# Second-layer weights combined on chip, one block product spread over the pairs, and pairs in another order

## The chip, the cores and the metric

The kernel runs on one core of a Trainium2 chip. The metric is the device time of one execution in microseconds (us); the time before is the median of three runs.

## What is computed

The reference chains three blocks on inputs of 4 batches with 576 positions each. Only the last one is touched by the change.

```python
def _moe2_ref(x, g_ln, w_ch1, w_ch2):          # x: (4, 576, 512)
    mu = np.mean(x, axis=-1, keepdims=True)
    var = np.mean((x - mu) ** 2, axis=-1, keepdims=True)
    xn = (x - mu) / np.sqrt(var + 1e-06) * g_ln
    ch = np.maximum(xn @ w_ch1, 0.0) @ w_ch2   # (512, 2048) and (2048, 512)
    return (x + ch).astype(np.float32)
```

Ahead of it come attention (8 heads, four of them with a local mask of 32 positions, four with a strided one) and a gated block with its own two products, `_attn_ref` and `_moe_ref`.

## The kernel before

**Stages.** The first 302 us are attention and the gated block, batch by batch. In the last batch, the hooks `PREP_AT` and `NORM0_AT` already prepare weights and normalise the first columns of the channel block. Then `last_stage` does the channel block in three thirds of 768 columns (`sc` = 0, 1, 2), each cut into two halves of 384 columns (`TH`).

**Precision.** Every f32 operand of a matmul is split in two parts, high and low (`split`: ScalarE writes the high part, VectorE the rest), and each product takes three matmuls, low by high, high by low, high by high.

**The first layer** is not done as eight block products of 2 by 2 blocks but as seven, on sums and differences of blocks (`expand` makes those of x, `combine` those of the weights). One pass is a *pair* i = 0 to 7: seven products of 6 matmuls each. In the first two thirds, `pair` does them in the order 1, 7, 6, 2, 5, 3, 4. Products 1, 6, 5 and 3 add up in one PSUM bank `a`, and ScalarE copies that bank out in between (`s1` after 1, `u2` after 6, `u4` after 5, `late(f1)` after 3): so product 6 waits for the copy `s1`, 5 for `u2`, 3 for `u4`. Bank `b` takes 7 and then 4, which waits for VectorE to have read 7 (`late(f2)`, L899); bank `c` takes 2. Three banks of a ring of four serve a pair.

**The second layer** of the first two thirds is `ch2`: 4 blocks of 3 matmuls, 12 for each f = 0 to 15. The first half's `ch2` are mixed into the pairs, the second half's follow as a loop of 16 on what `late` keeps. In the last third, `last_pair` only makes the sums (`hb`), and `last_chunk` does the second layer as seven block products too, of 48 matmuls each, in the order `ORDER2`; `grain` splits the inputs of a product, `fetch2` loads its two weight slices of 1024 KB, `out2` takes its results out.

**Weights.** `prepare(n)` runs the next n units of a list: `piece` loads and converts a quarter of the weights of one i (`from_f64`, in the staging tile `stg`), `combine` makes the seven sums of the first layer's weights and splits them into the tile `w1`, `second` splits the second layer's into `w2`, and `store2` writes the f32 copy of the latter to DRAM (`w2f_scratch`). `keep` writes `w1` to DRAM for the other two thirds, `fetch` reads it back into one of two tiles, used in turn. During the second third `combine2(i)` reads the f32 copy back into `stg`, makes the sums (L681 to L684), splits them and writes both parts to DRAM (L688) for `fetch2`.

**Order.** All loads and stores go through SyncE's one queue. The framework plans each engine's order when the kernel is built, from an estimate of costs and from who waits for whom, so an engine's order in the trace is near that of the source but not the same: what is ready may be drawn forward. On the chip each queue is then in that order.

Of the kernel before, what the change touches and what calls it, by code (L numbers as in the profile page):

```python
# [24 lines left out]
P = 128  # L25
# [19 lines left out]
WX2 = {1: (0, 2, 0), 2: (4, 2, 2), 7: (1, 2, 1), 4: (5, 2, 2), 5: (8, 1, 0), 6: (10, 1, 1), 3: (12, 1, 3)}  # L45
ORDER2 = (1, 2, 7, 6, 5, 4, 3)
XTAGS = (0, 4, 1, 5, 2, 3, 6)
# [104 lines left out]
def mixer_kernel(ctx: ExitStack, tc: tile.TileContext, io, out):  # L152
    nc = tc.nc
    y_d = nc.dram_tensor("y_scratch", (KD, P, NT), F32, kind="Internal").ap()
    w_d = nc.dram_tensor("w_scratch", (len(PRE), P, WP), F32, kind="Internal").ap()
    w2f_d = nc.dram_tensor("w2f_scratch", (NW, P, 2 * DM), F32, kind="Internal").ap()
    w2_d = nc.dram_tensor("w2_scratch", (14, P, NW, 2, P), F32, kind="Internal").ap()
# [511 lines left out]

    def store2(i):  # L670
        nc.sync.dma_start(out=w2f_d[i], in_=big["stg"][:, 2048:3072].bitcast(F32))

    def combine2(i):
        stg = big["stg"]
        c = stg[:, 0:1792].bitcast(F32)
        wf = c[:, 0:1024].rearrange("p (k e r f) -> p k e r f", k=2, e=2, r=2)
        nc.sync.dma_start(out=c[:, 0:1024], in_=w2f_d[i])
        s = c[:, 1024:1792].rearrange("p (s e f) -> p s e f", s=3, e=2)
        a11, a21, a12, a22 = wf[:, 0, :, 0], wf[:, 0, :, 1], wf[:, 1, :, 0], wf[:, 1, :, 1]
        tt = nc.vector.tensor_tensor  # L680
# [24 lines left out]
    for i in range(NW):  # L705
# [5 lines left out]
        if i + 1 < NW:  # L711
            units += [(combine, (i + 1,))]
        units += [(store2, (i,))]
    done = [0]
# [49 lines left out]
    def norm(sc, step, role):  # L764
# [21 lines left out]
        if step < 5:  # L786
            srs[sc] = col_sum(sc, (step - 1) % 2, step > 2)
        else:
            for k in range(KD):
                nc.scalar.activation(yc[:, k, :], yc[:, k, :], AF.Copy, scale=g_2[:, k:k + 1])  # L790

# [87 lines left out]
    def pair(sc, i, role, mid):  # L879
# [7 lines left out]
        product(sc, i, b, 7, True)  # L887
        product(sc, i, a, 6, False)
        u2 = tmp("u2")
        nc.scalar.activation(u2, a, AF.Copy)  # L890
        c = bank(role, "ps_p2")[:, :TH]
        product(sc, i, c, 2, True)
        c11 = tmp("c11")
        tt(out=c11, in0=c, in1=s1, op=ALU.add)
        h1 = to_h(c11)
        product(sc, i, a, 5, False)
        u4 = tmp("u4")
        nc.scalar.activation(u4, a, AF.Copy)
        tt(out=late(f2), in0=b, in1=u4, op=ALU.add)  # L899
        if i:  # L900
            ch2(sc, 0, f1 - 2, 1 - role)
        mid()
        product(sc, i, a, 3, False)
        nc.scalar.activation(late(f1), a, AF.Relu)
# [3 lines left out]
        h2 = to_h(c21)  # L908
        if i:
            ch2(sc, 0, f2 - 2, 1 - role)  # L910
# [7 lines left out]
    def last_stage():  # L918
        for sc in range(NSC - 1):
            role = sc % 2  # L920
            for i in range(NW):
                pair(sc, i, role, lambda: steps_at(sc, i - 0.5, role))
                if sc == 0:
                    if i + 2 < NW:
                        prepare(len(units[done[0]:]) if i + 3 == NW else 7)
                        if i < NW - 2:
                            keep(i + 2)
                else:
                    if i + 2 < NW:
                        fetch(i + 2)  # L930
                    combine2(i)
                steps_at(sc, i, role)
# [10 lines left out]
            for f in range(NF):  # L943
# [3 lines left out]
                if f == 4:  # L947
                    residual(sc, 1)
                ch2(sc, 1, f, role)
            for d in range(KD):  # L950
# [8 lines left out]

    def last_pair(sc, i, b):  # L960
        tt = nc.vector.tensor_tensor
        relu = lambda dst, src: nc.scalar.activation(dst, src, AF.Relu)
        a = bank8("ps_p1")[:, :TH]
        product(sc, i, a, 1, True)
        s1 = tmp("s1")
        nc.scalar.activation(s1, a, AF.Copy)
        o = bank8("ps_p6")[:, :TH]
        product(sc, i, o, 6, True)
        u2 = tmp("u2")
        tt(out=u2, in0=o, in1=s1, op=ALU.add)  # L970
        product(sc, i, a, 2, False)
        relu(b[:, 0], a)
        d = bank8("ps_p7")[:, :TH]
        product(sc, i, d, 7, True)
        u3 = tmp("u4")
        tt(out=u3, in0=d, in1=u2, op=ALU.add)
        c = bank8("ps_p5")[:, :TH]
        product(sc, i, c, 5, True)
        tt(out=b[:, 3], in0=c, in1=u3, op=ALU.add)
        relu(b[:, 3], b[:, 3])  # L980
        e = bank8("ps_p4")[:, :TH]
        product(sc, i, e, 4, True)
        tt(out=b[:, 2], in0=u3, in1=e, op=ALU.add)
        relu(b[:, 2], b[:, 2])
        product(sc, i, c, 3, False)
        tt(out=b[:, 1], in0=c, in1=u2, op=ALU.add)
        relu(b[:, 1], b[:, 1])

# [16 lines left out]
    def last_chunk(sc):  # L1005
# [3 lines left out]
        for i in range(NW):  # L1009
# [8 lines left out]
            b = hb[g][:, i % 2]  # L1018
            last_pair(sc, i, b)
            x = first_a[:, 2 * i:2 * i + 2] if 2 * i < NLATE else first_b[:, 2 * i - NLATE:2 * i - NLATE + 2]  # L1020
# [6 lines left out]
            if i + 2 < NW:  # L1027
                fetch(i + 2)
            if i in (1, 3):
                fetch2(i // 2)  # L1030
            if i == NW - 3:
                residual(sc, 0)
            if i >= NW - 2:
                rsqrt(sc, i + 2 - NW)
        pair_tile = lambda: big["h"].tile([P, 2, TH], F32R, tag="h", name="pt").bitcast(F32)
        ps, s1, u2, u3 = {}, pair_tile(), pair_tile(), pair_tile()
        for n, m in enumerate(ORDER2):
            if n + 1 < len(ORDER2):
                for e in range(2):
                    fetch2(2 * n + 2 + e)  # L1040
                for g in range(NW // 2):
                    grain(ORDER2[n + 1], g)
            onto = {2: 1, 3: 5}.get(m)
            for e in range(2):
                ps[m, e] = ps[onto, e] if onto else bank8("ps_c")[:, :TH]
            order = [(i, e) for i in range(NW) for e in range(2)]
            if n + 1 == len(ORDER2):
                order.sort(key=lambda ie: ie[1])
            for i, e in order:
                w, x = slices[m, e], grans[m, i]  # L1050
                for k, (a, c) in enumerate(((1, 0), (0, 1), (0, 0))):
                    nc.tensor.matmul(ps[m, e], lhsT=w[:, i, a, :], rhs=x[:, c, :], start=not onto and i == 0 and k == 0,  # L1052
                                     stop=i == NW - 1 and k == 2, skip_group_check=True)
                if i == NW - 1:
                    out2(sc, m, e, ps[m, e], s1[:, e], u2[:, e], u3[:, e])

    p7 = {}

    def out2(sc, m, e, o, s1, u2, u3):
        tt = nc.vector.tensor_tensor  # L1060

        def finish(half, r, src):
# [126 lines left out]
    open_d()  # L1189
    prepare(max(0, 14 - done[0]))  # L1190
    keep(1)
# [18 lines left out]
```

## Time and profile before

| | us |
|---|---|
| median of 3 runs (lowest, highest) | 695.57 (693.05, 697.37) |
| the profiled execution: its time, its span | 693.15, 691.0 |
| PE busy, PEld busy | 660.8, 626.8 |
| DVE busy, ACT busy | 507.7, 376.1 |
| mean share of the DMA queue in its 16 engines | 63.3% |

PE is TensorE's matmuls, PEld its weight loads, DVE VectorE, ACT ScalarE, SP SyncE with the DMA queue. The span is the time from the first to the last instruction; some 2 us of the execution's time lie around it. A matmul's row shows its whole way through the array, so that PE counts as busy also where one matmul starts later than it could; the spacing of starts tells more.

### The profile page before, as it was taken

Reading aid. Unit: us, or ns where it says so; the run is one execution under the profiler, and the core shown is the slowest. Engines: PE = TensorE matmul, PEld = TensorE weight load, DVE = VectorE, ACT = ScalarE, POOL = GpSimd, SP = SyncE. Lnnn points to the kernel's source line nnn. Section 1 sums busy time; section 2 is a strip of 40 time slices with the busy share of each in tenths; the row PEclk is TensorE's granted clock in tenths of the full one; section 3 lists DMA queues with packets and bytes.
Section 4 is the critical chain, followed back from the end, with each engine's and each line's share of the span. In section 5 each row is a group of like instructions: output and inputs, shape, how many; then the busy total and the mean of one; then the engine's idle time right before and its main releaser. Section 6 shows DMA issues by size and latency. Waiting matters only on the chain.

```text
span 691.0 us, 12856 instructions
## 1 busy us (share of the span) xinstructions
PE 660.8 (96%) x5002; PEld 626.8 (91%) x5002; DVE 507.7 (73%) x1026; ACT 376.1 (54%) x884; POOL 19.8 (3%) x24
## 2 busy tenths in 40 slices
PE   5899999999999998999999799989999999999997
PEld 4689989989888988999999699989999999999997
DVE  4889786586758686997798994564669757659683
ACT  3988967283568347646567743333476325445340
POOL 0011020000200020000000000000000000000000
PEclk9999999999999999999999999999999999999999
DMA  8863233557451650458978957799768869564753
GB/s 266 290 195 114 83 99 112 158 157 223 149 157 47 204 171 1 168 206 318 376 285 319 345 203 231 229 328 314 244 225 291 267 211 349 215 229 176 269 223 138
DMA packets 68235, 148.33 MB, mean 215 GB/s; under 512 B 4496, under 2 KB 43664, under 8 KB 63312
## 3 DMA queue, kind: packets, MB, share of 16 engines
q1 hardware_dynamic: 68176, 147.53, 63.3%
q8 instruction: 39, 0.64, 0.4%
q14 instruction: 20, 0.16, 0.1%
HBM read 101.90 MB, written 45.61 MB: 213 GB/s over the span
## 4 chain that ended last, share of the span: by engine, by line
PE 55%; DVE 15%; DMA 13%; ACT 11%; issue 3%; POOL 1%; SPq 1%; DVEq 0%; ACTq 0%; POOLq 0%
PE ps_p L833 19%; PE ps_c L1052 7%; PE ps_o L208 4%; PE ps_o L209 4%; PE ps_o L210 4%; DMA w<-w_scratch 2%; DMA w_scratch<-w_p 2%; ACT pt L405 2%; DMA qk<-in_qk_l 2%; DMA w_scratch<-stg 2%; DMA stg<-in_w_ch 2%; PE ps_y L208 2%; PE ps_y L210 1%; PE ps_y L209 1%; PE ps_t L444 1%
## 5 line engine op out<-in xcount | busy, mean ns | idle before, releaser
L833 PE MATMUL ps_p<-x,w 128*128 128x384 f32 x1008 | 187.8, 339 | 8.3 <-DVE w L185 3.6
L833 PEld LDWEIGHTS ps_p<-x,w 128*128 128x128 f32 x1008 | 175.1, 189 | 14.8 <-DVE w L185 3.9
L209 PE MATMUL ps_o<-h,w2p 128*128 128x384 f32 x192 | 64.3, 335 | 0.0
L210 PE MATMUL ps_o<-h,w2p 128*128 128x384 f32 x192 | 64.2, 334 | 0.0
L208 PE MATMUL ps_o<-h,w2p 128*128 128x384 f32 x192 | 62.3, 335 | 0.4 <-ACT h L838 0.4
L1052 PE MATMUL ps_c<-t,w2c 128*128 128x384 f32 x288 | 50.5, 335 | 1.1 <-DMA w2c<-w_scratch 1.0
L1052 PEld LDWEIGHTS ps_c<-t,w2c 128*128 128x128 f32 x288 | 49.9, 188 | 1.7 <-DMA w2c<-w_scratch 1.3
L208 PE MATMUL ps_g<-wsg,vn 128*128 128x288 f32 x128 | 39.0, 305 | 0.0
L210 PE MATMUL ps_g<-wsg,vn 128*128 128x288 f32 x128 | 38.2, 299 | 0.0
L208 PE MATMUL ps_u<-xhl,winl 128*128 128x288 f32 x128 | 38.1, 297 | 0.0
L208 PE MATMUL ps_y<-gt,wout 128*128 128x288 f32 x128 | 37.9, 298 | 0.1
L209 PE MATMUL ps_g<-wsg,vn 128*128 128x288 f32 x128 | 37.9, 296 | 0.0
L209 PE MATMUL ps_u<-xhl,winh 128*128 128x288 f32 x128 | 37.8, 295 | 0.0
L210 PE MATMUL ps_u<-xhl,winh 128*128 128x288 f32 x128 | 37.7, 295 | 0.0
L210 PE MATMUL ps_y<-gt,wout 128*128 128x288 f32 x128 | 37.5, 295 | 0.0
L209 PE MATMUL ps_y<-gt,wout 128*128 128x288 f32 x128 | 37.5, 294 | 0.0
L208 PEld LDWEIGHTS ps_o<-h,w2p 128*128 128x128 f32 x192 | 35.8, 188 | 0.7 <-ACT h L838 0.7
L209 PEld LDWEIGHTS ps_o<-h,w2p 128*128 128x128 f32 x192 | 36.0, 188 | 0.4 <-DVE h L839 0.2
L210 PEld LDWEIGHTS ps_o<-h,w2p 128*128 128x128 f32 x192 | 36.1, 188 | 0.0
L838 ACT ACTIVATE h<-late 128x384 fp32r<-128x384 f32 x32 | 16.7, 524 | 35.1 <-PE ps_o L210 30.5
L184 ACT ACTIVATE t<-hb 128x768 fp32r<-128x768 f32 x24 | 20.2, 846 | 23.5 <-PE ps_c L1052 23.0
L208 PE MATMUL ps_v<-winh,xhl 128*128 128x512 f32 x80 | 31.9, 399 | 0.3 <-DVE xhl L500 0.2
(225 smaller groups left out, 1574.4 us busy)
## 6 DMA issues: line engine op xcount, KB each, us to landing
w<-w_scratch SPq DMA_DIRECT2D x16, 1792.0 KB, 7.7
w_scratch<-w SPq DMA_DIRECT2D x8, 1792.0 KB, 7.6
w_scratch<-stg SPq DMA_DIRECT2D x16, 896.0 KB, 6.3
w2c<-w_scratch SPq DMA_DIRECT2D x14, 1024.0 KB, 6.2
stg<-in_w_ch SPq DMA_DIRECT2D x22, 512.0 KB, 6.0
raw_p<-in_w_ch SPq DMA_DIRECT2D x20, 256.0 KB, 3.1
qk<-in_qk_s SPq DMA_DIRECT2D x8, 601.0 KB, 4.5
y_scratch<-y SPq DMA_DIRECT2D x16, 288.0 KB, 3.1
```

The lines of the kernel that those rows point to most:

```text
L184: nc.scalar.activation(dst_h, src, AF.Copy)
L208: nc.tensor.matmul(ps, lhsT=ll, rhs=rh, start=first, stop=False)
L209: nc.tensor.matmul(ps, lhsT=lh, rhs=rl, start=False, stop=False)
L210: last_mm[0] = nc.tensor.matmul(ps, lhsT=lh, rhs=rh, start=False, stop=last)
L405: exps.append(nc.scalar.activation(p3[:, i, :], src, AF.Exp, scale=SCALE, bias=mx[:, i:i + 1], accum_out=sm[:, i:i + 1]))
L444: nc.tensor.transpose(ps[:rows, (t - t0) * c:(t - t0 + 1) * c], src, ident)
L833: nc.tensor.matmul(o, lhsT=w[:, a, n0 + nk * k, :], rhs=x[:, c, k, :], start=first and k == 0 and n == 0, stop=k == 1 and n == 2, skip_gro ...
L838: nc.scalar.activation(h[:, 0, :], src, AF.Relu)
L1052: nc.tensor.matmul(ps[m, e], lhsT=w[:, i, a, :], rhs=x[:, c, :], start=not onto and i == 0 and k == 0, stop=i == NW - 1 and k == 2, skip_g ...
```

## The change

It has five parts. (1) `w2f_scratch` and `store2` are gone; `combine2` adds the high and the low part of `w2[i]` on VectorE instead of loading the sum; as `store2` was one unit of seven in each step, `prepare` counts 6 and 13. `combine2(7)` moves from pair 7 of the second third into the loop of its second half, at f = 12 (`COMBINE_F`). (2) `pair` takes the products in the order 1, 7, 2, 6, 5, 3, 4 and puts one `ch2` before 5 and the other before 3, in place of one before 3 and one after 4; in pair 7 the second stays at the end. (3) `last_pair` takes the scheme of `pair`, with one bank for four products. (4) In the last third, block product 1 of the second layer is no longer a stage of 48 matmuls but goes in 6 at a time, inside the next pair (`mid`, between 5 and 3); the stage after it is product 7, whose slices come one after the other, then 2. Banks come from `bank6`, and `fetch2(0)` and `fetch2(1)` stand after pair 0. (5) The scaling by `g_2` in the first third's normalisation goes from ScalarE to VectorE.

```diff
-ORDER2 = (1, 2, 7, 6, 5, 4, 3)
+COMBINE_F = {12: 7}
+ORDER2 = (1, 7, 2, 6, 5, 4, 3)
...
-    def store2(i):
-        nc.sync.dma_start(out=w2f_d[i], in_=big["stg"][:, 2048:3072].bitcast(F32))
-
     def combine2(i):
         stg = big["stg"]
         c = stg[:, 0:1792].bitcast(F32)
         wf = c[:, 0:1024].rearrange("p (k e r f) -> p k e r f", k=2, e=2, r=2)
-        nc.sync.dma_start(out=c[:, 0:1024], in_=w2f_d[i])
+        w = w2[i].rearrange("p a k f -> p a (k f)").bitcast(F32)
+        nc.vector.tensor_tensor(out=c[:, 0:1024], in0=w[:, 0], in1=w[:, 1], op=ALU.add)
...
-        units += [(store2, (i,))]
...
             for k in range(KD):
-                nc.scalar.activation(yc[:, k, :], yc[:, k, :], AF.Copy, scale=g_2[:, k:k + 1])
+                if sc:
+                    nc.scalar.activation(yc[:, k, :], yc[:, k, :], AF.Copy, scale=g_2[:, k:k + 1])
+                else:
+                    nc.vector.tensor_scalar_mul(yc[:, k, :], yc[:, k, :], g_2[:, k:k + 1])
...
         product(sc, i, b, 7, True)
-        product(sc, i, a, 6, False)
-        u2 = tmp("u2")
-        nc.scalar.activation(u2, a, AF.Copy)
         c = bank(role, "ps_p2")[:, :TH]
         product(sc, i, c, 2, True)
         c11 = tmp("c11")
         tt(out=c11, in0=c, in1=s1, op=ALU.add)
+        product(sc, i, a, 6, False)
+        u2 = tmp("u2")
+        nc.scalar.activation(u2, a, AF.Copy)
         h1 = to_h(c11)
+        if i:
+            ch2(sc, 0, f1 - 2, 1 - role)
         product(sc, i, a, 5, False)
         u4 = tmp("u4")
         nc.scalar.activation(u4, a, AF.Copy)
         tt(out=late(f2), in0=b, in1=u4, op=ALU.add)
-        if i:
-            ch2(sc, 0, f1 - 2, 1 - role)
         mid()
+        if 0 < i < NW - 1:
+            ch2(sc, 0, f2 - 2, 1 - role)
         product(sc, i, a, 3, False)
...
-        if i:
+        if i == NW - 1:
             ch2(sc, 0, f2 - 2, 1 - role)
...
-                    combine2(i)
+                    if i < NW - len(COMBINE_F):
+                        combine2(i)
...
+                if sc and f in COMBINE_F:
+                    combine2(COMBINE_F[f])
                 ch2(sc, 1, f, role)
...
+    def bank6(name):
+        bank_turn[0] += 1
+        if bank_turn[0] % 3 == 0:
+            return ps_a.tile([P, 512], F32, tag="a", name=name)
+        return ps_d.tile([P, 512], F32, tag="d", name=name)
...
-            last_pair(sc, i, b)
+            last_pair(sc, i, b, lambda: step2(1, i - 1))
...
-            if i in (1, 3):
-                fetch2(i // 2)
+            if i == 0:
+                fetch2(0)
+                fetch2(1)
...
+        for g in range(NW // 2):
+            grain(ORDER2[1], g)
+        step2(1, NW - 1)
         for n, m in enumerate(ORDER2):
             if n + 1 < len(ORDER2):
                 for e in range(2):
                     fetch2(2 * n + 2 + e)
-                for g in range(NW // 2):
-                    grain(ORDER2[n + 1], g)
...
+                if n:
+                    for g in range(NW // 2):
+                        grain(ORDER2[n + 1], g)
+            if n == 0:
+                for e in range(2):
+                    out2(sc, 1, e)
+                continue
             order = [(i, e) for i in range(NW) for e in range(2)]
-            if n + 1 == len(ORDER2):
+            if n + 1 == len(ORDER2) or n == 1:
                 order.sort(key=lambda ie: ie[1])
             for i, e in order:
...
+    def step2(m, i, es=(0, 1)):
+        for e in es if i >= 0 else ():
+            if i == 0:
+                ps[m, e] = bank2(m, e)
+            w, x = slices[m, e], grans[m, i]
+            for k, (a, c) in enumerate(((1, 0), (0, 1), (0, 0))):
+                nc.tensor.matmul(ps[m, e][:, :TH], lhsT=w[:, i, a, :], rhs=x[:, c, :], skip_group_check=True,
+                                 start=m not in (2, 3) and i == 0 and k == 0, stop=i == NW - 1 and k == 2)
```

The new `last_pair`, in full (its lines that fall away are those printed above):

```python
    def last_pair(sc, i, b, mid):
        tt = nc.vector.tensor_tensor
        relu = lambda dst, src: nc.scalar.activation(dst, src, AF.Relu)
        a = bank6("ps_p1")[:, :TH]
        product(sc, i, a, 1, True)
        s1 = tmp("s1")
        nc.scalar.activation(s1, a, AF.Copy)
        o = bank6("ps_p7")[:, :TH]
        product(sc, i, o, 7, True)
        product(sc, i, a, 6, False)
        u2 = tmp("u2")
        nc.scalar.activation(u2, a, AF.Copy)
        c = bank6("ps_p2")[:, :TH]
        product(sc, i, c, 2, True)
        tt(out=b[:, 0], in0=c, in1=s1, op=ALU.add)
        relu(b[:, 0], b[:, 0])
        product(sc, i, a, 5, False)
        u4 = tmp("u4")
        nc.scalar.activation(u4, a, AF.Copy)
        tt(out=b[:, 3], in0=o, in1=u4, op=ALU.add)
        relu(b[:, 3], b[:, 3])
        mid()
        product(sc, i, a, 3, False)
        relu(b[:, 1], a)
        product(sc, i, o, 4, False)
        tt(out=b[:, 2], in0=o, in1=u2, op=ALU.add)
        relu(b[:, 2], b[:, 2])
```

## Rows read from the trace of the kernel before

**Rows 1.** The page: busy time of the engines, share of the span, instructions.

```profile
PE 660.8 (96%) x5002; PEld 626.8 (91%) x5002; DVE 507.7 (73%) x1026; ACT 376.1 (54%) x884; POOL 19.8 (3%) x24
```

**Rows 2.** Waits of PE, whole span: us in total, times, longest.

```profile
PE ps_p L833 <- DVE w L185: 3.6, 1, 3.6
...
PE ps_p L833 <- ACT u L898: 2.4, 2, 1.8
...
PE ps_p L833 <- DMA w<-w_scratch: 1.2, 2, 0.8
PE ps_c L1052 <- DMA w2c<-w_scratch: 1.0, 1, 1.0
...
PE ps_p L833 <- ACT s L885: 0.3, 1, 0.3
```

**Rows 3.** Timeline of PE: a dense stretch of the last third.

```profile
626.87 5.36 PE L1052 MATMUL ps_c<-t_a,w2c 128*128 128x384 f32 x30
```

**Rows 4.** Timeline of PE around pair 7 of the first third.

```profile
384.47 0.34 PE L210 MATMUL ps_o<-h,w2p 128*128 128x384 f32 x1
388.42 3.01 PE L833 MATMUL ps_p<-x,w 128*128 128x384 f32 x12 [3.61 <-DVE w L185]
391.75 4.14 PE L833 MATMUL ps_p<-x,w 128*128 128x384 f32 x18 [0.33 <-ACT s L885]
396.47 1.31 PE L833 MATMUL ps_p<-x,w 128*128 128x384 f32 x6 [0.58 <-ACT u L898]
```

**Rows 5.** Stretches: length; busy PE, PEld, DVE, ACT, POOL; clock, DMA share, GB/s.

```profile
384.64:397.62 12.98, 8.46 (x37) 7.47 (x37) 12.46 (x20) 9.34 (x16) 0.00 (x0) 0.87 0.98 394
```

**Rows 6.** The same view, the part of that stretch at the lower clock.

```profile
390.10:393.60 3.50, 3.17 (x11) 2.67 (x10) 3.43 (x6) 3.10 (x5) 0.00 (x0) 0.54 0.98 418
```

**Rows 7.** Timeline ahead of pair 7: loads, conversion and split of its weights.

```profile
372.32 1.87 SPq L193 DMA_DIRECT2D stg<-in_w_ch  x2
...
378.60 0.67 ACT L197 ACTIVATE stg<-stg 128x512 f32<-128x512 f32 x1
...
380.75 0.69 ACT L197 ACTIVATE stg<-stg 128x512 f32<-128x512 f32 x1
...
386.33 2.03 DVE L185 TENSOR_TENSOR w<-stg,w 128x1792 fp32r<-128x1792 f32 x1
```

**Rows 8.** Timeline of ACT ahead of that: its idle time before the conversion of pair 6.

```profile
369.56 0.53 ACT L184 ACTIVATE sr<-o 128x384 fp32r<-128x384 f32 x1 [2.92 <-DVE o L753]
369.99 0.66 ACT L197 ACTIVATE stg<-stg 128x512 f32<-128x512 f32 x1
```

**Rows 9.** DMA issues: KB each, median us from issue to landing.

```profile
w<-w_scratch SPq DMA_DIRECT2D x16, 1792.0 KB, 7.7
...
w2f_scratch<-stg SPq DMA_DIRECT2D x8, 512.0 KB, 5.9
```

**Rows 10.** Timeline of ACT in pair 1 of the second third.

```profile
450.42 1.70 ACT L184 ACTIVATE stg<-stg 128x1792 fp32r<-128x1792 f32 x1 [2.88 <-DVE stg L684]
...
452.44 0.47 ACT L898 ACTIVATE u<-ps_p 128x384 f32<-128x384 f32 x1
```

**Rows 11.** Groups of DVE from 302 us on: busy us, mean ns, idle before, releaser.

```profile
L185 DVE TENSOR_TENSOR w2p<-stg,w2p 128x1024 fp32r<-128x1024 f32 x6 | 7.3, 1220 | 0.9 <-ACT w2p L184 0.9
...
L681 DVE TENSOR_TENSOR stg<-stg 128x256 f32<-128x256 f32 x8 | 3.4, 420 | 5.3 <-DMA stg<-w2f_scratch 5.3
```

**Rows 12.** Stretch of the second third, columns as in rows 5.

```profile
436.54:567.38 130.84, 129.00 (x737) 127.36 (x737) 84.16 (x147) 58.57 (x101) 0.00 (x0) 1.00 0.84 270
```

**Rows 13.** Line L681: ns min/median/max, first and last start.

```profile
L681 DVE TENSOR_TENSOR stg<-stg x8: 413/420/426, 415.3 to 555.1; 128x256 f32<-128x256 f32 x8
```

**Rows 14.** Line L701, its slices: us to landing.

```profile
DMA to landing us min/median/max: 4.6/6.2/8.0
```

**Rows 15.** Waits of SP, whole span: us in total, times, longest.

```profile
SPq L677 <- DMA w_scratch<-stg: 14.9, 7, 6.0
```

**Rows 16.** Line L688, the stores of the sums: us to landing.

```profile
DMA to landing us min/median/max: 4.7/6.3/10.4
```

More of the change, by code (lines that the diff above doesn't have):

```diff
@@ L155, in mixer_kernel @@
     w_d = nc.dram_tensor("w_scratch", (len(PRE), P, WP), F32, kind="Internal").ap()
-    w2f_d = nc.dram_tensor("w2f_scratch", (NW, P, 2 * DM), F32, kind="Internal").ap()
     w2_d = nc.dram_tensor("w2_scratch", (14, P, NW, 2, P), F32, kind="Internal").ap()
@@ L924, in last_stage @@
                     if i + 2 < NW:
-                        prepare(len(units[done[0]:]) if i + 3 == NW else 7)
+                        prepare(len(units[done[0]:]) if i + 3 == NW else 6)
                         if i < NW - 2:
@@ L958, in bank8 @@
         return bank(bank_turn[0] % 2, name)
-    def last_pair(sc, i, b):
+    def bank6(name):
[4 more added lines that the diff above has]
+    def last_pair(sc, i, b, mid):
         tt = nc.vector.tensor_tensor
         relu = lambda dst, src: nc.scalar.activation(dst, src, AF.Relu)
-        a = bank8("ps_p1")[:, :TH]
+        a = bank6("ps_p1")[:, :TH]
         product(sc, i, a, 1, True)
@@ L966, in last_pair @@
         nc.scalar.activation(s1, a, AF.Copy)
-        o = bank8("ps_p6")[:, :TH]
-        product(sc, i, o, 6, True)
+        o = bank6("ps_p7")[:, :TH]
+        product(sc, i, o, 7, True)
+        product(sc, i, a, 6, False)
         u2 = tmp("u2")
[L970 to L979, printed above, removed]
-        relu(b[:, 3], b[:, 3])
-        e = bank8("ps_p4")[:, :TH]
-        product(sc, i, e, 4, True)
-        tt(out=b[:, 2], in0=u3, in1=e, op=ALU.add)
+        nc.scalar.activation(u2, a, AF.Copy)
+        c = bank6("ps_p2")[:, :TH]
+        product(sc, i, c, 2, True)
+        tt(out=b[:, 0], in0=c, in1=s1, op=ALU.add)
+        relu(b[:, 0], b[:, 0])
+        product(sc, i, a, 5, False)
+        u4 = tmp("u4")
+        nc.scalar.activation(u4, a, AF.Copy)
+        tt(out=b[:, 3], in0=o, in1=u4, op=ALU.add)
+        relu(b[:, 3], b[:, 3])
+        mid()
+        product(sc, i, a, 3, False)
+        relu(b[:, 1], a)
+        product(sc, i, o, 4, False)
+        tt(out=b[:, 2], in0=o, in1=u2, op=ALU.add)
         relu(b[:, 2], b[:, 2])
-        product(sc, i, c, 3, False)
-        tt(out=b[:, 1], in0=c, in1=u2, op=ALU.add)
-        relu(b[:, 1], b[:, 1])
     grain_turn = [0]
@@ L1034, in last_chunk @@
                 rsqrt(sc, i + 2 - NW)
-        pair_tile = lambda: big["h"].tile([P, 2, TH], F32R, tag="h", name="pt").bitcast(F32)
-        ps, s1, u2, u3 = {}, pair_tile(), pair_tile(), pair_tile()
+        for g in range(NW // 2):
+            grain(ORDER2[1], g)
+        step2(1, NW - 1)
         for n, m in enumerate(ORDER2):
@@ L1040, in last_chunk, with bank2, out2 @@
                     fetch2(2 * n + 2 + e)
-                for g in range(NW // 2):
-                    grain(ORDER2[n + 1], g)
-            onto = {2: 1, 3: 5}.get(m)
-            for e in range(2):
-                ps[m, e] = ps[onto, e] if onto else bank8("ps_c")[:, :TH]
+                if n:
[5 more added lines that the diff above has]
+                continue
             order = [(i, e) for i in range(NW) for e in range(2)]
-            if n + 1 == len(ORDER2):
+            if n + 1 == len(ORDER2) or n == 1:
                 order.sort(key=lambda ie: ie[1])
             for i, e in order:
[L1050 to L1053, printed above, removed]
+                step2(m, i, (e,))
                 if i == NW - 1:
-                    out2(sc, m, e, ps[m, e], s1[:, e], u2[:, e], u3[:, e])
+                    out2(sc, m, e)
+    ps = {}
+    def bank2(m, e):
+        if m == 1:
+            return ps_s.tile([P, 512], F32, tag="s", name="ps_c")
+        if m in (2, 3):
+            return ps[{2: 1, 3: 5}[m], e]
+        return bank6("ps_c")
+    def step2(m, i, es=(0, 1)):
[6 more added lines that the diff above has]
+                                 start=m not in (2, 3) and i == 0 and k == 0, stop=i == NW - 1 and k == 2)
+    sums = {}
     p7 = {}
-    def out2(sc, m, e, o, s1, u2, u3):
+    def out2(sc, m, e):
         tt = nc.vector.tensor_tensor
+        if not sums:
+            for n in ("s1", "u2", "u3"):
+                sums[n] = big["h"].tile([P, 2, TH], F32R, tag="h", name="sum").bitcast(F32)
+        o = ps[m, e][:, :TH]
+        s1, u2, u3 = (sums[n][:, e] for n in ("s1", "u2", "u3"))
         def finish(half, r, src):
@@ L1189, in mixer_kernel @@
     open_d()
-    prepare(max(0, 14 - done[0]))
+    prepare(max(0, 13 - done[0]))
     keep(1)
```

## The prediction

> **What bounds the kernel now.** The page first: PE is busy 660.8 us, 96% of the span [rows 1], and the change leaves every matmul in place. So the time can only move by what TensorE waits, and the next view is the list of PE's waits [rows 2]: from 302 us on, the reader is to see one of 3.6 us for a weight split of VectorE, 2.4 us for ScalarE's copy `u4` (L898), 1.2 us for `fetch`ed weights, 1.0 us for slices of the second layer. To know what a wait costs, I take the spacing of dense matmuls: 30 in 5.36 us, less the 0.34 us that one is on its way, is 5.02 / 29 = 0.173 us [rows 3, 4]. Six take 1.04 us, twelve 2.08.
>
> The dearest place is pair 7 of the first third. Between 384.64 and 397.62 TensorE does 36 matmuls, 6.2 us of work, in 12.98 us [rows 4, 5]: 6.7 us are lost. 3.6 us of it is the wait for the split of this pair's weights; then, from 390.10 to 393.60, the granted clock averages 0.54, that is nearly all at 1.2 GHz, and 11 matmuls take 3.5 us instead of 1.9 [rows 6]; the rest is two waits for ScalarE's copies. The DMA queue is busy 0.98 of this stretch [rows 5].
>
> **The change part by part.** *Part 1, no `store2`, no load in `combine2`.* Eight stores and eight loads of 512 KB fall away, 8.4 MB. Where it can count is ahead of pair 7. The chain there: two loads issued from 372.32 on, converted by ScalarE at 378.60 and 380.75, summed, split by VectorE at 386.33 for 2.03 us, and TensorE starts at 388.42 [rows 4, 7]. The loads can only go once the conversion of pair 6's pieces has freed their slots, and that conversion writes where `store2(5)` was still reading. What a 512 KB store less ahead of them is worth has two ends: its bytes at the stretch's 394 GB/s, 0.52 MB / 394 = 1.3 us [rows 5], or its whole landing, 5.9 us [rows 9], of which no more than the 3.6 us of the wait can come back; below, nothing, if the chain is held by something else (ScalarE was idle 2.92 us for VectorE just before that conversion [rows 8]). I take 2.5, the middle of 1.3 and 3.6. The slow clock followed that wait. With a wait of 1.1 us left I count 1.0 of its 1.6 us (3.5 − 11 × 0.173) as gained; ends 0 and 1.6. The Trainium skill (TensorE: Matmul & The Clock Gate, section "The HAM clock gate") says that idleness drops the clock to half and activity brings it back. The rows agree on the first; by that rule a short wait would leave the clock alone, and the sum would be 0.6 us lower.
>
> In the second third, the one wait over 1 us is in pair 1: `u4` at 452.44 stood behind the 1.70 us split of `combine2`, which ScalarE could only begin at 450.42 [rows 10], since VectorE's sums had waited for the load; such waits were 5.3 us in four times [rows 11]. Now the sum's input is on chip. Gain 1.6 of the 1.8 us [rows 2]; ends 0 and 1.8. The price is one add of 128x1024 per i; VectorE's split of the same shape took 1.22 us [rows 11], so 8 × 1.22 = 9.8 us on an engine that is busy 84.2 of 130.8 us there [rows 12]. Its cover is the 2.08 us of `ch2` that stands behind each copy; I count nothing, and what it costs without cover is the third rival. The moved `combine2(7)` (now five sums, two splits, two stores) began its sums at 555.1 [rows 13]. The second half ends at 567.4 [rows 12] after 16 × 2.08 us, so f = 12 begins at 567.4 − 4 × 2.08 = 559.1. From there 1.22 + 4 × 0.42 + 1.70 + 2.03 us [rows 7, 10, 11] and a landing of 6.3 [rows 16] make 572.0, and the slice of product 1 that SyncE fetches behind it is there 6.2 us later [rows 14], at 578.2. It is first needed in pair 1, after 42 and 30 matmuls, at 567.4 + 12.5 = 579.9. Nothing, with 1.7 us to spare.
>
> *Part 2, the new order of `pair`.* Between 1 and 6 now lie 12 matmuls instead of 6: the copy `s1` (0.33 us of wait in pair 7 [rows 4], 0.5 with the half-idle start after it) no longer ends a wait. Gain 0.5, ends 0 and 0.5. From pair 1 to pair 6, each of 6 to 5 and 5 to 3 has 12 matmuls of `ch2` between. Uncovered are 6 to 5 in pair 0 of both thirds (no `ch2` yet; product 1 of the next pair can be drawn forward) and 5 to 3 in pair 7 of the second third. An uncovered copy cost 0.58 us in pair 7 [rows 4]. I count two of these three, 1.2 us; ends 0 and 1.7.
>
> *Parts 3 and 4, the last third.* A pair now holds 48 matmuls, 8.3 us, instead of 42, 7.3. `fetch(i+2)` can go when pair i is done and takes 7.7 us [rows 9]: so far it is late when anything is ahead of it, 1.2 us in two waits [rows 2]; now it has 0.6 us to spare. Gain 1.2, ends 0 and 1.2. `fetch2(0)` and `fetch2(1)` stand earlier in the source, but go out when `combine2(7)` has landed, as before; they share the queue ahead of `fetch(2)`. Nothing. `last_pair` now has two more copies of ScalarE in TensorE's way, `u2` with product 2 behind it and `u4` with the 6 matmuls of `mid`: 0.47 us for such a copy [rows 10] under a cover of 1.04. The nearest row is `s1` in `pair` before, with the same cover: 0.3 us in one of 16 [rows 2]. With 16 such places and a fuller ScalarE I count 0.7; ends 0 and 16 × 0.33 = 5.3. Then the stage after the pairs: the second slice of product 7 goes into a tile that pair 7 reads to its end, and is needed 6 + 24 matmuls later, after 5.2 us. A slice lands 4.6 to 8.0 us after its issue, 6.2 in the middle [rows 14]; the queue is empty there, so nearest is the low end: I count 0.3, ends 0 and 2.8. The Trainium skill (DMA: Bandwidth & Descriptors, section "Anatomy of one DMA") gives 2.0 us plus bytes at 436 GB/s, an estimate of 4.4 us for 1.05 MB. By it this term is nil, below any row. The 1.0 us wait for a slice two stages later [rows 2] stays: stores of results stand before that slice in the queue as they did.
>
> *Part 5* moves four scalings from ScalarE to VectorE in a stage where PE's list has no wait of theirs: nothing, either way.
>
> Sum: −2.5 − 1.0 − 1.6 − 0.5 − 1.2 + 1.2 + 0.7 + 0.3 = −4.6 us. Of the profiled execution's 693.15 us that leaves 688.5; it is 2.4 below the median of the runs, so against the median I forecast 695.57 − 4.6 = **691.0 us**. About 1%, 7 us, is what a measurement of this kernel can tell from no change; the bounds are 688.6 and 702.5.
>
> **The rivals.** *The place at pair 7 closes altogether.* For it: its queue is at 0.98, and the loads stand behind the bytes removed. Against: ScalarE's idle 2.92 us there has another cause. It gives back 3.6 + 1.6 + 0.5, with 1.8, 1.2 and the slice's 1.0, and the new edges cost nothing: −9.7, 685.9 us.
>
> *The change doesn't reach the wait.* The conversion ahead of pair 7 is held by ScalarE's and VectorE's order, not by the store; the 3.6 us and the slow clock stay, and the hidden load was hidden anyway. For it: rows 8. Then −0.5 − 1.2 − 0.3 (part of the second third) + 2.2 = +0.2: 695.8 us.
>
> *VectorE waits in SyncE's stead (slower).* The first sum of `combine2` overwrites what the stores of the one before still read. So far SyncE waited for that landing, 14.9 us in seven times, the longest 6.0 [rows 15]; now the add itself does, with `c21`, the low part of `h` and `late` behind it on VectorE, and TensorE behind these. It decides from the point where the wait is longer than the cover of 2.08 us. If the add is placed right behind the split before it, it waits 6.3 us [rows 16] and TensorE loses 4.2; three of seven cost 12.6: 703.6 us. Against: a pair lasts 11.4 us (66 × 0.173), so that the stores have landed if the add is placed a pair later. The Trainium skill (TensorE: Matmul & The Clock Gate, section "Architectural detail") says that VectorE's queue is strictly first in, first out; by that rule nothing can pass a waiting add. No row here shows one passing.
>
> **How the numbers follow.** The forecast 0.45, its own range 688 to 694; the closed place 0.24; not reached 0.21; slower 0.10. Faster by over 1%: 0.24 and 0.08 of the forecast's low side, 0.32. Slower by over 1%: 0.10. Within: 0.58. The range takes in the first three cases with their unknowns (below, the second half of the slow clock and the slices; above, half of the ScalarE copies' 5.3 us): 684 to 699. Left out are the slower case and some 0.05 at either end.
>
> **What will show it.** In PE's waits: the split of `w` falls from 3.6 to about 1 us, and the stretch of lower clock with it; `u` (L898's successor) in the second third and `w<-w_scratch` vanish. New rows would be `u` and `s` copies in the last third and a slice early in its second layer. The `w2f_scratch` lines are gone from the DMA issues, 8 adds of some 1.2 us are new. Wrong I am if the wait at pair 7 is still above 3 us (not the store), or if VectorE shows waits of several us for `w_scratch<-stg`.

## The result, and the profile after

The changed kernel takes 685.11 us in the median of four executions (683.51 to 685.95), beside 694.51 us of the kernel before on the same chip. The ratio is 0.986 (0.982 to 0.990): 9.4 us less, where the forecast against that median was 4.6. Measured a second time (below), it was 0.983 (0.980 to 0.987). The gain is nearest to the first rival's, the place at pair 7 closing altogether, which gave 9.7 us and had a chance of 0.24.

The page of the changed kernel, busy times and moved data; TensorE has the 5002 matmuls of [rows 1]:

```profile
PE 661.6 (97%) x5002; PEld 630.5 (92%) x5002; DVE 507.5 (74%) x1022; ACT 378.7 (55%) x896; POOL 19.4 (3%) x24
...
DMA packets 65931, 139.94 MB, mean 205 GB/s; under 512 B 4240, under 2 KB 43408, under 8 KB 61008
```

Its list of PE's waits (total, times, longest), which answers to [rows 2]. The reader is to see what is not there: no `w` of VectorE and no `w` of a fetch; and `h`, which was one wait of 0.4 us before and is now 1.4 us in two.

```profile
PE ps_o L208 <- ACT h L838: 1.4, 2, 0.7
...
PE ps_p L833 <- ACT u L900: 0.5, 2, 0.3
PE ps_c L1083 <- DMA w2c<-w_scratch: 0.5, 1, 0.5
PE ps_p L833 <- ACT u L894: 0.4, 1, 0.4
...
PE ps_p L833 <- DVE late L901: 0.3, 1, 0.3
PE ps_p L833 <- ACT u L989: 0.2, 1, 0.2
```

The timeline of PE around pair 7 of the first third, for [rows 4]. The three waits come to 0.8, 0.6 and 0.8 us, start to start; none is for the weights.

```profile
383.95 0.62 PE L208 MATMUL ps_o<-h,w2p 128*128 128x384 f32 x2 [0.67 <-ACT h L838]
384.41 3.28 PE L833 MATMUL ps_p<-x,w 128*128 128x384 f32 x18
...
390.88 1.31 PE L833 MATMUL ps_p<-x,w 128*128 128x384 f32 x6 [0.40 <-ACT u L894]
...
397.21 0.97 PE L208 MATMUL ps_o<-h,w 128*128 128x384 f32 x4 [0.68 <-ACT h L838]
```

The same stretch as a window, for [rows 5, 6]: 67 matmuls instead of 37 in 13 us, the granted clock at 1.00, the queue at 0.60 instead of 0.98.

```profile
384.41:397.50 13.09, 12.00 (x67) 11.16 (x66) 12.73 (x22) 11.80 (x20) 0.00 (x0) 1.00 0.60 227
```

To place all of the gain, I cut the last 2103 matmuls in three by their number (705, 736 and 662: first, second and last third) and take from each stretch its matmuls at the dense 0.1733 us [rows 3]. What is left is what TensorE lost, in us, in the profiled execution of each kernel of this study:

| kernel | first | second | last third | sum |
|---|---|---|---|---|
| before (from 304.73, 436.54, 567.38, to 686.79) | 9.6 | 3.3 | 4.7 | 17.6 |
| after (from 307.51, 433.13, 562.85, to 679.95) | 3.4 | 2.2 | 2.4 | 8.0 |
| 1 part 1 | 3.9 | 5.8 | 4.5 | 14.2 |
| 2 part 2 | 9.7 | 1.3 | 8.4 | 19.4 |
| 3 parts 3, 4 | 9.4 | 5.0 | 3.1 | 17.5 |
| 4 store from the parts | 9.3 | 4.6 | 4.5 | 18.4 |
| 5 small store | 5.3 | 6.0 | 4.9 | 16.1 |
| 6 store by GpSimd | 12.2 | 4.9 | 4.3 | 21.4 |
| 7 yc load late | 8.0 | 7.3 | 4.6 | 20.0 |
| 8 yc load early | 9.5 | 3.1 | 7.1 | 19.7 |
| 9 after again | 4.0 | 3.2 | 3.4 | 10.5 |
| 10 after without part 2 | 2.6 | 3.9 | 3.4 | 9.9 |
| 11 after without part 5 | 5.4 | 3.3 | 2.3 | 11.1 |
| 12 after, old pair 7 | 3.6 | 2.9 | 2.8 | 9.3 |

The profiled span fell by less than 9.6 us, by 6.8 (691.0 to 684.2), since the changed kernel began this stretch 2.8 us later; ahead of it, from 12 to 60 us, its granted clock averaged 0.93, that of the kernel before 1.00.

Two profiled executions of the changed kernel differ by 1.0 us in a third and by 2.5 in the sum. In the last third the eight kernels with the old one lose 4.3 to 8.4 us, the six with the new one 2.3 to 3.4. The two highest, 2 and 8, have a wait for fetched weights there of 2.7 and 1.9 us, and behind it ten matmuls at a spacing of 0.32 us instead of 0.17, at a granted clock of 0.50 and 0.54: some 1.5 us more. A wait for a copy of ScalarE, 2.7 and 2.3 us, with the same behind it stands in the second third of kernels 1 and 3. So a single profile says little of effects under 2 us in the later thirds. The first third is steadier, 9.3 to 9.7 us in five kernels that keep the 512 KB stores in SyncE's queue, and it carries the result: −6.2 of −9.6 us.

### The profile page after: what moved, and what is told of

The parts are those of the page before. It is cut to its first block, busy times and chain, and to the rows that moved or that the text cites. A ratio compares the mean times of both kernels' runs of the same rounds, so it can differ in the third digit from the quotient of the medians.

```text
span 684.2 us, 12814 instructions
## 1 busy us (share of the span) xinstructions
PE 661.6 (97%) x5002; PEld 630.5 (92%) x5002; DVE 507.5 (74%) x1022; ACT 378.7 (55%) x896; POOL 19.4 (3%) x24
## 4 chain that ended last, share of the span: by engine, by line
PE 61%; DVE 13%; ACT 12%; DMA 10%; issue 2%; SPq 1%; POOL 1%; ACTq 0%; DVEq 0%; POOLq 0%
PE ps_p L833 16%; PE ps_c L1083 8%; PE ps_o L208 5%; PE ps_o L209 5%; PE ps_o L210 5%; DMA w_scratch<-w_p 3%; PE ps_g L208 2%; PE ps_g L210 2%; PE ps_g L209 2%; ACT pt L405 2%; PE ps_t L444 2%; PE ps_y L208 2%; PE ps_y L210 2%; PE ps_y L209 2%; PE ps_pv L463 1%
## 5 line engine op out<-in xcount | busy, mean ns | idle before, releaser
L833 PE MATMUL ps_p<-x,w 128*128 128x384 f32 x1008 | 184.9, 336 | 1.6 <-ACT u L900 0.5
L208 PE MATMUL ps_o<-h,w2p 128*128 128x384 f32 x192 | 63.6, 335 | 0.7 <-ACT h L838 0.7
L209 PE MATMUL ps_v<-winl,xhl 128*128 128x512 f32 x80 | 31.7, 396 | 0.0
```

The source lines that it names most:

```text
L208: nc.tensor.matmul(ps, lhsT=ll, rhs=rh, start=first, stop=False)
L209: nc.tensor.matmul(ps, lhsT=lh, rhs=rl, start=False, stop=False)
L833: nc.tensor.matmul(o, lhsT=w[:, a, n0 + nk * k, :], rhs=x[:, c, k, :], start=first and k == 0 and n == 0, stop=k == 1 and n == 2, skip_gro ...
```

## The experiments

Times are ratios to the kernel before on the same chip, with the 95% interval.

**1, 2 and 3: the parts alone.**

Each takes the lines of its part from the diff above and nothing else; their cores are

```diff
-        units += [(store2, (i,))]
...
-        nc.sync.dma_start(out=c[:, 0:1024], in_=w2f_d[i])
+        nc.vector.tensor_tensor(out=c[:, 0:1024], in0=w[:, 0], in1=w[:, 1], op=ALU.add)
```

```diff
-        product(sc, i, a, 6, False)
...
         c = bank(role, "ps_p2")[:, :TH]
         product(sc, i, c, 2, True)
...
+        product(sc, i, a, 6, False)
```

```diff
-    def last_pair(sc, i, b):
+    def last_pair(sc, i, b, mid):
...
+            last_pair(sc, i, b, lambda: step2(1, i - 1))
```

> Part 1 alone on the kernel before: the stores of the f32 copies dropped, combine2 adds the parts on chip, the old order of pair and the old last third. The stores' theory (they stand ahead of the loads for pair 7 of the first third, as the prediction has it): the wait of 3.6 us for the split of w falls below 1, no stretch at half clock follows it (together some 5 us back), and u4 in pair 1 of the second third loses its wait of 1.8: some 688.5 us. The order's theory (it is the new order of pair that lets ScalarE and VectorE convert and split earlier): the wait at pair 7 stays above 3 us, only the 1.8 us come back: some 693 us.

> Part 2 alone: only the order of products in pair is the new one; stores, loads and the last third are those of before. The stores' theory: the wait at pair 7 stays above 3 us with the half clock behind it; 0.5 us for s1 comes back, the uncovered copies cost about as much: 694 to 696 us. The order's theory: the split of w comes some 4 us earlier and the place closes: some 690 us.

> Parts 3 and 4 alone: only the last third is the new one. The prediction's terms (1.2 back at the fetches, 0.7 and 0.3 for ScalarE's copies and the slice) give 0.2 us less, 694.3 us, with waits of 0.7 us or more for copies in the last third. If instead the copies lie under cover, as the changed kernel's trace suggests (TensorE lost 2.4 us there after 561 us from the start, 4.7 before the change), 2.3 us come back: 692.2 us. Pair 7 of the first third is untouched and keeps its 3.6 us.

Measured: part 1 0.990 (0.986 to 0.993), part 2 1.001 (0.998 to 1.004), parts 3 and 4 0.997 (0.995 to 0.999). With part 2 and with parts 3 and 4 the wait of 3.6 us for `w` stays; with part 1 it is 0.3 us and the first third loses 5.7 us less. So part 1 closes the place, by the removal of the stores or by what goes with it, and the new order has no share in it. Parts 3 and 4 fit the second reading, 2.3 us, better than the forecast's 0.2. The product of the three, 0.988, is near the whole, 0.986.

But part 1 alone pays in the second third. Its timelines of VectorE, ScalarE and TensorE there:

```profile
464.43 1.23 DVE L675 TENSOR_TENSOR stg<-w2p 128x1024 f32<-128x1024 f32 x1 [2.96 <-DMA w_scratch<-stg]
...
467.28 1.70 ACT L184 ACTIVATE stg<-stg 128x1792 fp32r<-128x1792 f32 x1 [3.84 <-DVE stg L682]
468.88 0.47 ACT L887 ACTIVATE u<-ps_p 128x384 f32<-128x384 f32 x1
...
469.41 2.11 PE L830 MATMUL ps_p<-x,w 128*128 128x384 f32 x6 [2.74 <-ACT u L887]
```

The new add on VectorE waits 2.96 us for the stores of the `combine2` before; sums and ScalarE's split come late with it, `u2` stands behind the split, and TensorE waits 2.74 us; then come matmuls at half pace (granted clock 0.52 from 469.5 to 473.0 us). That is the prediction's slower rival, link by link, once instead of three times.

**4: the bytes without the hold.** Is it that the store still reads the buffer which the next conversion overwrites?

On top of kernel 1:

```diff
     def store2(i):
-        nc.sync.dma_start(out=w2f_d[i], in_=big["stg"][:, 2048:3072].bitcast(F32))
+        nc.sync.dma_start(out=w2f_d[i], in_=w2[i][:, 0].rearrange("p k f -> p (k f)").bitcast(F32))
```

> Part 1, but with a store of 512 KB kept at the place of each old one; it reads the high part of the second weights, and nobody reads what it writes. So the bytes go as before, but no store reads the buffer that the next conversion overwrites. If the hold on that buffer made the wait at pair 7, the wait falls below 1 us as in part 1 alone: some 689 us. If it was the bytes ahead in a queue that is busy 0.98, the wait stays at 2.5 us or more, with the half clock behind it: some 692 to 693 us.

Measured: 1.000 (0.997 to 1.003), all of the gain gone, the wait for `w` at 3.6 us again:

```profile
PE ps_p L835 <- DVE w L186: 3.6, 1, 3.6
```

So the wait doesn't need that hold. Bytes were still possible, but the timelines of SyncE showed two more differences. First, in the kernel before each of the first five pairs of loads below stands right behind a store, and the store waits until both pieces of the round before are converted, though the first piece's slot is free sooner. Second, with other instructions to place, the framework put the 1.5 MB load of `yc` at another point of SyncE's queue. The timeline of SyncE in the kernel before, stores (L671), loads of pieces (L193) and `yc` (the sixth round is [rows 7]):

```profile
307.45 2.55 SPq L193 DMA_DIRECT2D stg<-in_w_ch  x2
...
320.91 2.39 SPq L193 DMA_DIRECT2D stg<-in_w_ch  x2
...
328.96 0.43 SPq L768 DMA_DIRECT2D yc<-y_scratch  x1
331.98 0.32 SPq L671 DMA_DIRECT2D w2f_scratch<-stg  x1
332.41 2.68 SPq L193 DMA_DIRECT2D stg<-in_w_ch  x2
...
349.71 0.32 SPq L671 DMA_DIRECT2D w2f_scratch<-stg  x1
350.14 1.20 SPq L193 DMA_DIRECT2D stg<-in_w_ch  x2
...
361.53 0.32 SPq L671 DMA_DIRECT2D w2f_scratch<-stg  x1
361.96 2.43 SPq L193 DMA_DIRECT2D stg<-in_w_ch  x2
```

And in the changed kernel:

```profile
306.81 2.55 SPq L193 DMA_DIRECT2D stg<-in_w_ch  x2
309.45 1.19 SPq L765 DMA_DIRECT2D yc<-y_scratch  x1
...
319.31 1.88 SPq L193 DMA_DIRECT2D stg<-in_w_ch  x2
...
333.24 2.47 SPq L193 DMA_DIRECT2D stg<-in_w_ch  x2
...
344.08 1.85 SPq L193 DMA_DIRECT2D stg<-in_w_ch  x2
...
356.72 1.63 SPq L193 DMA_DIRECT2D stg<-in_w_ch  x2
...
366.79 9.99 SPq L193 DMA_DIRECT2D stg<-in_w_ch  x3
```

Each round can go when the one before is converted, so the six form a chain: 307.45 to 372.32, that is 64.9 us, before; 306.81 to 366.79, 60.0, after. The longest round takes 17.7 us before, the one behind `yc`, and 13.9 after, which is 3.8 of the 4.9 us. The last round takes 10.4 and 10.1 us: nothing to speak of came off there. The next four kernels take the chain apart.

**5 to 8: queue, bytes and the place of the yc load.**

Kernels 5 to 7 are kernel 1 with one more edit each (5 and 6 keep `store2`), kernel 8 is the kernel before with one.

```diff
-        nc.sync.dma_start(out=w2f_d[i], in_=big["stg"][:, 2048:3072].bitcast(F32))
+        nc.sync.dma_start(out=w2f_d[i, :, 0:64], in_=big["stg"][:, 2048:2112].bitcast(F32))
```

```diff
-        nc.sync.dma_start(out=w2f_d[i], in_=big["stg"][:, 2048:3072].bitcast(F32))
+        nc.gpsimd.dma_start(out=w2f_d[i], in_=big["stg"][:, 2048:3072].bitcast(F32))
```

In 7, `load` is the load of `yc` in `norm` and `kept[0]` the last store of `keep`:

```diff
+                tc.add_manual_dep(load.ins, kept[0].ins.name, ORDER, reason="place of the load")
```

```diff
-NORM_AT = ({1: (0,), 3: (1,), 3.5: (2,), 4.5: (3,), 5: (4,), 6: (5,)},
+NORM_AT = ({0: (0,), 3: (1,), 3.5: (2,), 4.5: (3,), 5: (4,), 6: (5,)},
```

> Part 1, with a store of 32 KB kept at the place of each old one of 512 KB: it waits for the same conversion and stands at the same place in SyncE's queue, and nobody reads what it writes. In this build the planner puts the 1.5 MB load of yc behind the third pair of loads, as in part 1 alone, not after the fourth store of w as in the kernel before. Three readings of what made the split for pair 7 of the first third late. Bytes: the 512 KB of each store in the DMA queue; then the wait is gone here. The queue: loads of the next pieces stand behind a store that waits for both pieces to be converted, though the first of their slots is free 1.5 to 2 us earlier; then some 2 us of the 3.6 stay. The place of the yc load: 1.5 MB ahead of the loads of a late round (landing 11.7 us in the kernel before, 8.2 in part 1 alone); then the wait is gone here.

> Part 1, but with the old stores of 512 KB kept, issued by GpSimd's queue instead of SyncE's (nobody reads what they write). Bytes as before and the staging tile held as before, but no load stands behind a store, and the yc load is placed early. Bytes: the wait of 3.6 us at pair 7 stays at 2.5 or more. The queue: it falls by 2 or more. The place of the yc load: it falls below 1.

> Part 1, no stores at all, but the 1.5 MB load of yc is bound to come after the fourth store of w, its place in the kernel before. Bytes of the stores or their place in the queue: the wait at pair 7 is gone as in part 1 alone, 689 us. The place of the yc load: the wait comes back with 2.5 us or more and the half clock behind it, some 694 us.

> The kernel before with one number changed: the load of yc belongs to pair 0 instead of pair 1, so that it stands one round of loads earlier in SyncE's queue, after the third store of w. All stores stay. Bytes or queue: the wait of 3.6 us at pair 7 stays above 2.5, time as before. The place of the yc load: it falls below 1.5 and the half clock goes, some 5 us less, 691 us.

Measured: 5 0.994 (0.991 to 0.996); 6 1.005 (1.001 to 1.008); 7 0.998 (0.994 to 1.002); 8 0.999 (0.996 to 1.002). The chains, from the first round's loads to the sixth's, read as above:

| kernel | stores in SyncE's queue | yc load | chain, us |
|---|---|---|---|
| before | 512 KB, from `stg` | late | 64.9 |
| 8 | the same | one round earlier | 64.9 |
| 4 | 512 KB, not from `stg` | late | 63.6 |
| 5 | 32 KB | early | 61.7 |
| 7 | none | late | 61.2 |
| 1 | none | early | 59.7 |
| 6 | none (GpSimd's, 512 KB) | early | 66.8 |

What follows. *The place of the yc load* alone does nothing (8: its own round becomes the long one, 17.3 us, and nothing is caught up later), and with no stores it is 1.5 us of chain (7 against 1). *The place of a store in the queue*, at 32 KB, is 2.0 us (5 against 1). The rest, the bytes of 512 KB, is not measured by itself: 5 and 4 differ by 1.9 us, but in the place of `yc` too, and 5 and 8 by 3.2 us with `yc` early in both, but not at the same place. So no one cause was the whole; my two-way readings were too plain, and 5 came out between them (wait 0.5 us for `w`, 1.5 for `h`).

In 6, moving the store to another queue was worse: nothing keeps the loads behind the store any more, so a conversion now does wait for the store that reads its buffer, and it stands on ScalarE ahead of TensorE's copies. ScalarE's waits there, total, times, longest:

```profile
ACT stg L198 <- DMA w2f_scratch<-stg: 4.7, 2, 2.4
```

In 7 the chain is 3.7 us shorter than before, shorter too than in 5, but TensorE still waits 3.3 us, now for `h`. ScalarE's timeline of 7 says why: the four sums of the weights are done at 384.63, but their split begins at 386.20, behind a scaling of `yc`, `rb` and the load of an activation table; and `h` stands behind the split and two conversions.

```profile
382.46 0.94 ACT L791 ACTIVATE yc<-yc,g 128x768 f32<-128x768 f32 x1
...
384.47 1.28 ACT L796 ACT_TABLE_LOAD   x1
385.77 0.53 ACT L796 ACTIVATE o<-rb 128x384 f32<-128x384 f32 x1
386.20 1.68 ACT L184 ACTIVATE w<-stg 128x1792 fp32r<-128x1792 f32 x1
387.78 1.21 ACT L197 ACTIVATE stg<-stg 128x512 f32<-128x512 f32 x2
388.90 0.51 ACT L839 ACTIVATE h<-c 128x384 fp32r<-128x384 f32 x1
```

**9 to 12: parts in the company of the others.**

9 is the changed kernel itself, 10 has the old `pair` everywhere, 11 and 12 change a place each (in 12, `pair_old` is the old `pair`):

```diff
-                    nc.vector.tensor_scalar_mul(yc[:, k, :], yc[:, k, :], g_2[:, k:k + 1])
+                    nc.scalar.activation(yc[:, k, :], yc[:, k, :], AF.Copy, scale=g_2[:, k:k + 1])
```

```diff
-                pair(sc, i, role, lambda: steps_at(sc, i - 0.5, role))
+                (pair_old if sc == 0 and i == NW - 1 else pair)(sc, i, role, lambda: steps_at(sc, i - 0.5, role))
```

> The changed kernel itself, beside the three that follow: 685 us, ratio 0.986 to the kernel before. It is the yardstick for what they lose or gain.

> The changed kernel with the old order of pair (part 2 undone). If the parts add up, nothing changes against the changed kernel, since part 2 alone changed nothing (ratio 1.001). If the new order is the cover for the add that part 1 puts on VectorE, a wait of some 3 us for u2 in the second third appears, where VectorE's add waits for the stores of the combine2 before and ScalarE's 1.70 us split stands ahead of u2, as in the run of part 1 alone (TensorE lost 5.8 us in the second third there, 2.2 in the changed kernel); against it 1.7 us come back around pair 7: some 687 us, 0.3% more than the changed kernel.

> The changed kernel with part 5 undone: the scalings of yc by g_2 on ScalarE again. As the prediction has it, nothing, 685 us. If ScalarE's order still sets when pair 7's weights are ready (in the run with the late yc load its split of w stood behind four scalings of 0.93 us and an activation-table load), the wait at pair 7 grows by 1 to 3 us: 686 to 688 us.

> The changed kernel with the old order of products in pair 7 of the first third alone. In the changed kernel TensorE loses 2.9 us from 379 to 398 us, waiting three times for ScalarE; in the run of part 1 alone, with the old order, 1.2. If the order of that pair makes the difference, 1.7 us come back: 683.4 us. If it is that ScalarE is full there, nothing: 685 us.

Measured: 9 0.983 (0.980 to 0.987); 10 0.982 (0.978 to 0.985); 11 0.987 (0.984 to 0.990); 12 0.987 (0.982 to 0.991). The four intervals overlap. Against 9 itself, 10 and 12 are not told from nothing; 11 is 2.5 us slower in the median (688.5 against 686.0, six executions each), at the edge of what this tells. The profiles say a little more. Without part 2 (10) the second third loses 0.7 us more than in 9, in two waits for `u2`, each behind a split of `combine2` whose add had waited 1.3 to 1.4 us for stores:

```profile
468.35 1.31 PE L833 MATMUL ps_p<-x,w 128*128 128x384 f32 x6 [1.19 <-ACT u L890]
...
481.21 1.33 PE L833 MATMUL ps_p<-x,w 128*128 128x384 f32 x6 [0.97 <-ACT u L890]
```

and the first third 1.4 less. So the new order does take those waits, as expected; it seems to give as much back around pair 7, and the times show no gain in sum. In 12 the three waits at pair 7 stay as they are in the changed kernel (0.8, 0.6 and 0.8 us), so that pair's own order doesn't make them. But 1 and 10, with the old order in every pair, have none of the three, only 0.3 and 0.7 us for `w`, and ScalarE is busy 15.6 us of the 20 from 380 us on there, 17.0 to 18.4 in the changed kernel, 9, 11 and 12. So these waits go with the new order in the pairs ahead; how, no run shows.

Kernel 11 doesn't test what I wrote it for. The scalings that stand near pair 7 on ScalarE normalise the second third's columns, and part 5 doesn't move them; it moves four near 275 us. Both kinds in the changed kernel:

```profile
273.06 0.61 DVE L790 TENSOR_SCALAR n<-n,g 128x768 f32<-128x768 f32 x1
...
384.27 0.93 ACT L788 ACTIVATE yc<-yc,g 128x768 f32<-128x768 f32 x1
```

So whether ScalarE's scalings delay pair 7's weights stays untested, and pair 7 in 11 is as in 9. What differs is a wait of TensorE for VectorE's `c` in pair 0 of the first third. The ten kernels without part 5 have it, with 0.2 to 1.0 us, the four with it don't; the kernel before and 11:

```profile
PE ps_p L833 <- DVE c L894: 0.7, 1, 0.7
```

```profile
PE ps_p L830 <- DVE c L888: 1.0, 1, 1.0
```

No version here is clearly faster than the changed kernel.

## Why the prediction was right, and where its sizes were off

Its sign held, and so did its whole range, 684 to 699. But its sum was half of the gain, and the forecast's own range, 688 to 694, was missed: the whole range holds 685.1 only because it takes in the first rival. By place that rival's terms came out too: 5.7 us for pair 7, where the first third lost 6.2 less; 1.8 for `u4`, 1.1 in the second third; 2.2 for fetches and slices, 2.3 in the last. That its sum is within 0.3 us is in part luck, as it counted no new waits and there are some.

**The wait at pair 7**, −2.5 of 3.6 forecast, is gone. Kernel 1 shows that the place closes without the stores, as forecast. What failed is the place, and with it the size, in the step "What a 512 KB store less ahead of them is worth has two ends": it asked how much earlier the last loads go when one store less is ahead of them, and took 2.5 us. But no store held that last round: the one issued ahead of it, at 361.53, had landed 5.2 us later, 3 us before the conversion at 369.99 that the loads waited for, and the round takes as long without stores (10.4 us before, 10.5 in kernel 1). The loads of pair 7 end a chain of six rounds, each of which waits for the one before, and the gain came off earlier ones, most of it off the one behind `yc`: 64.9 us become 59.7 in kernel 1, 60.0 in the changed kernel. Counted from where TensorE begins the first third in the table, the sixth round goes out after 67.6 us before and after 59.3 in the changed kernel. That covers the 3.6 us of wait whole. The hold on `stg` that the step named beside the bytes is not what the wait needs: without it (4) the chain is 1.3 us shorter and the wait as long. ScalarE's idle 2.92 us [rows 8], named against the closing, didn't keep the place open; that ScalarE's order can do so, the timeline of kernel 7 suggests.

**The slow clock**, −1.0 of 1.6, went with the wait: the granted clock is 1.00 from 379 to 398 us, though three matmuls in that stretch come 0.6 to 0.8 us late. By the Trainium skill's rule that the prediction weighed (TensorE: Matmul & The Clock Gate, section "The HAM clock gate") the sum was 0.6 us lower, and this trace agrees with it.

**Part 2**: `s1` no longer ends a wait, as forecast (−0.5). The uncovered copies were put at pair 0 and at one 5 to 3, +1.2 us. At pair 0 no wait shows. At 5 to 3 there are waits in pairs 6 and 7 of the second third (0.5 and 0.4 us), the first of them behind a cover of 12 matmuls. The rest is in pair 7 of the first third, 0.6 us for `u2` and 0.8 twice for `h`, where the forecast had put nothing: 3.1 us in all. The forecast took covers from the order of products; in pair 7 that was not what counted (12), and ScalarE is fuller there than with the old order.

**`u4` in pair 1 of the second third**, −1.6: what is left there is 0.45 us for `late`, so some 1.4 came back. The add takes 1.22 us on the chip as VectorE's split of that shape did [rows 11]. That it costs nothing held, but with less room than forecast. The prediction named several us of VectorE's waits for `w_scratch<-stg` as a sign that it was wrong, and they are there. The waits of VectorE in the second third of the changed kernel:

```profile
DVE stg L675 <- DMA w_scratch<-stg: 6.2, 3, 3.1
```

TensorE paid 2.7 us for one such wait in kernel 1, 2.2 for two in kernel 10, and nothing that is seen in the changed kernel, where `ch2` stands between 6 and 5. As a sign the row was badly chosen: it decides only together with the cover behind it. The Trainium skill's rule that VectorE's queue is first in, first out (TensorE: Matmul & The Clock Gate, section "Architectural detail") agrees with the trace: in kernel 1 nothing of VectorE starts in the 2.96 us that the add waits.

**`combine2(7)`** was to begin at 559.1 us, so that its slice is there 1.7 us before it is needed. In the changed kernel, whose second third ends 4.5 us earlier, that place is near 554 us. Its add began at 539.7 (the last start of that line): the framework drew it forward.

```profile
L675 DVE TENSOR_TENSOR stg<-w x2: 1218/1218/1218, 386.3 to 539.7; 128x1024 f32<-128x1024 f32 x2
```

**The last third**, −0.2 in the forecast's sum (−1.2 + 0.7 + 0.3), lost 2.4 us instead of 4.7 (3.4 in run 9; 3.1 in kernel 3). The fetch waits are gone, the copies of ScalarE cost 0.4 and 0.3 us in two places, the 0.7 of the forecast. The second slice of product 7 was put at 0.3 and cost 0.5 us, 0.8 in run 9: it was issued at 628.35, landed 4.8 us later, and the matmul that reads it started at once. From the last six matmuls of product 1 on, the framework had placed it behind 25 others, not 30.

```profile
628.35 0.32 SPq L699 DMA_DIRECT2D w2c<-w_scratch  x1
...
633.18 46.93 PE L1083 MATMUL ps_c<-t,w2c 128*128 128x384 f32 x269 [0.53 <-DMA w2c<-w_scratch]
```

By the Trainium skill (DMA: Bandwidth & Descriptors, section "Anatomy of one DMA"), an estimate of 4.4 us for a slice, that term was nil. But the formula there is a fit to DMAs on GpSimd's path, and SyncE issues the slices; this slice took 4.8 us, and the 14 of the changed kernel land after 6.1 in the middle:

```profile
w2c<-w_scratch SPq DMA_DIRECT2D x14, 1024.0 KB, 6.1
```

The wait of 1.0 us for a slice two stages later, which was to stay, is gone.

**Part 5** was put at nothing. But TensorE's wait for `c` in pair 0, 0.7 us before, is in every kernel without it and in none with it, some 30 us behind the scalings that it moves. How these bear on it is not shown.

**What stays open**: how much of the chain is bytes and how much the place of `yc`, at full stores; what makes the three waits at pair 7; and whether parts 2 and 5 are worth a few tenths of a per cent.

## What to carry to other kernels

When a wait ends a chain of rounds that each need the one before, cost an edit over all the rounds, not over the last one; compare the time from the first round's issue to the last one's, and each round with the same one before. An edit that adds or removes an instruction in an order that a framework plans can move others that it never names: look where the large transfers went before putting a gain down to the bytes. A wait that moves from a queue to an engine is paid or not by the work that lies between the copy behind it and its reader, so judge such a wait and its cover together.

## What the runs showed of the hardware

In a busy queue the size of a store hardly set when it landed: 32 KB took 5.3 us in the median in kernel 5 (queue at 0.77 from 300 to 395 us), 512 KB 5.9 us before [rows 9] (0.86 from 300 to 390 us). The same 512 KB issued by GpSimd's queue took 8.7 us (kernel 6, 300 to 395 us):

```profile
w2f_scratch<-stg SPq DMA_DIRECT2D x7, 32.0 KB, 5.3
```

```profile
w2f_scratch<-stg POOLq DMA_DIRECT2D x7, 512.0 KB, 8.7
```

The granted clock fell to half behind waits of TensorE of 3.6 us (before), 2.7 (1 and 2), 2.3 (3) and 1.9 us (8), and not behind the wait of 1.8 us in the second third of the kernel before.
